# Attention on the FFN's array: two visits per batch through all eight PSUM banks, in place of three visits

## The chip, the cores and the metric

The kernel runs on one NeuronCore of one Trainium2 chip. The metric is device time in microseconds (us) for one execution of the whole program. The kernel before took 302.94 us, the median of three runs (301.93 to 303.04). Engines are named as the profile names them: PE is TensorE's matmul side and PEld its weight load, DVE is VectorE, ACT is ScalarE, POOL is GpSimd (which here only issues loads and a few memsets), and SP is SyncE (which issues transposing DMAs and stores).

## The reference

The inputs are q, k and v of shape (8 batches, 8 heads, 576 positions, 64), w_in (512 x 2048) and w_out (2048 x 512), all fp32; the output is (4608, 512) in fp32. Heads 0 to 3 look at the last 32 positions, heads 4 to 7 at every fourth of the last 128.

```python
scores = q @ k.T / sqrt(64)
rel = pos[:, None] - pos[None, :]
mask_plain = (rel >= 0) & (rel < 32)                        # heads 0 to 3
mask_dil = (rel >= 0) & (rel < 128) & (rel % 4 == 0)        # heads 4 to 7
attn = softmax(where(mask, scores, -1e9))
x = (attn @ v) with the heads side by side, one row per token: (4608, 512)
out = relu(x @ w_in) ** 2 @ w_out
```

## The kernel before

**Two jobs on one array.** Attention of batch b makes the token rows that the FFN (feed-forward network) reads later. Both run in one instruction stream, interleaved by hand: `groups` is the list of FFN groups, and after each group the program runs the attention steps that are due there. Tokens are kept by residue modulo 4 (`RES`), so that dilated heads become dense ones. Heads are handled in pairs e: pairs 0 and 1 are the near heads, pairs 2 and 3 the far (dilated) ones.

**The FFN.** `ffn_groups` cuts the tokens into blocks of 512 columns (the first four of 256). A block of 512 has 32 groups. In the first 16 (`mm1`, line 872) each group is four matmuls of 512 columns into one PSUM tile "pf"; ACT then takes Relu into h2T (line 885) and DVE squares it in place (line 886). In the last 16 (`g2`, line 914), sixteen matmuls for each of four row blocks of 128 tokens read h2T and fill another "pf"; ACT copies it to an `osb` buffer (line 920), of which there are three, and SP stores it (line 841). From group 64 on, the block that starts at group t = 32 (b - 1) is the one beside which batch b is worked on.

**Visits.** From batch `NATURAL` = 3 on, attention uses the array as four quadrants of 64 x 64, in one call of `quadrants` (matmuls at line 601), here called a visit. A visit is given a list `scs` of (batch, pair) whose scores it makes and a list `pvs` whose products with V and whose row sums it makes. It keeps one list of matmuls for each quadrant (g, c), g for the rows and c for the columns, and issues from the quadrant whose streamed columns are fewest. A step that ends in a visit is written `visit(at, scs, pvs)`: it runs after group `at`. Before, batch b has scores of pair 2 at t-8, scores of 3 and products of 2 at t+5, scores of 0 and 1 and products of 3 at t+17, and products of 0 and 1 (with scores of pair 2 of the next batch) at t+24. Batch 3 has them at groups 59, 71, 81 and 88.

**PSUM.** There are eight banks: four "pf" in rotation (`ps_f`, the FFN's), two "pa" (`ps_a`), one "po" and one "pd". A visit's first score pair goes to the two "pa", its first product pair to "po" and "pd"; a second pair of either kind borrows two "pf".

**Around a visit.** After the scores come the steps `E` (ACT's Exp at line 638, DVE's mask at line 640, the `sums` of neighbouring blocks at line 647); after the products `L` (ACT's Ln of the row sums, lines 614 to 620) and `X` (ACT's Exp of the negated Ln at line 624, DVE's multiplication into xT at lines 627 and 629). Before the scores, DVE arranges what arrived: `R` (lines 476 and 479) copies the far heads' block ends, `K` (line 470) and `Q` (line 468) copy the near heads.

**How data arrives.** POOL issues, in a written order (the `PROGRAM` string, then `LOAD_V`, `LOAD_QK`), loads of q and k (line 171, four DMAs a batch: two parts of each), and of V (lines 443, 448 and 455: 24 DMAs a batch, 16 of them rows of the near heads). SP issues four transposing DMAs a batch (`cross`, line 238) from the staged q and k to `qx` and `kx`, between the stores of the FFN. POOL uses eight DMA semaphores in rotation. Each engine works its queue in program order.

The step order within one group number is set by the second entry of the step's tuple; the program sorts on these two:

```python
steps.append((at, 2, b, "V0" + ...))            # a visit
steps.append(((57, 57, 54, 55)[x] if early else t - 14 + x, 1, b, code))   # R
steps.append((t + x if early else t - 6 + x, 1, b, code))                  # K, Q
...
while steps and steps[0][0] <= g:
    natural_step(*steps.pop(0)[2:])
```

Of the kernel before, what the change touches and what calls it, by code (L numbers as in the profile page):

```python
# [12 lines left out]
RES = 4  # L13
# [12 lines left out]
    "X21 M21 L31 X31 M31 E01 E11 | L2:q00123 L2:q10123 L1:v1dpr | | P01 D01 L01 X01 M01 P11 D11 L11 X11 M11 | | "  # L26
    "| | | | | | | | | | m n | | | | | | 1q1 1q3 | 1q2f 1k2f | 1k1a 1v3 | 1a2 | 1v2 1k0a 1q0v | 1o2 | 1a0 1a1 | "
    "1k3 1o0 1o1f | 1a3 1Q0 | 1K0 1o3 | 1Q1 1K1 | 1Q2 | 1b0 | | 1Q3 1K2 L2:vwp L3:q00123 L3:q10123 L2:vwdr | "
    "L2:x | | 2q0 | | 2k0 1V2 | 1b2 1p0 | 1b1 1V3 1K3 | L3:x | 1p2 1p1f | 2a0 1b3 | 2k1l 2b0 2o0 1p3f 2k1h | 2q1 "
    "| | 2p0 L3:V 2a1 | 2b1 | | 2o1 | | | 2p1f L4:q10123 L4:q00123 | | | | L4:x | | | | | | | | | | | | | | | | "  # L30
    "| | L4:V | | | | | | | | | | | L5:q10123 | | | | L5:q00123 | | L5:V | | | | | | L5:x | | | | | | | | "
    "L6:q00123 | | | | | | | | | | | | | L6:q10123"
# [32 lines left out]
def kernel(  # L65
# [109 lines left out]
    def crossed(b: int, e: int):  # L175

        return int(b == XB and e == 3 or b >= NATURAL and e == 1)
# [259 lines left out]
    def load_v_rows(b: int):  # L437


        vds[b] = vd_pool.tile([P, NE // 2, 2, RES * D], bf16, name="vd")  # L440
        for hl, rows in enumerate(sides):
            for e in range(NE // 2):
                nc.gpsimd.dma_start(  # L443
                    vds[b][rows, e, :, :],
                    v[b, H // 2 + 2 * e + hl, 0:512, :].rearrange("(m p r) d -> p m (r d)", p=64, r=RES),
                )
            for i in (0, 8):
                nc.gpsimd.dma_start(  # L448
                    v_rows[b % 2][rows, NE // 2 :, i, :],
                    v[b, H // 2 + hl : H : 2, 64 * i : 64 * i + 64, :].rearrange("h p d -> p h d"),  # L450
                )
            for e in range(NE // 2):
                p0 = sides[hl ^ crossed(b, e)].start
                for r in range(RES):
                    nc.gpsimd.dma_start(  # L455
                        v_rows[b % 2][p0 + 16 * r : p0 + 16 * r + 16, e, :, :],
                        v[b, 2 * e + hl, :, :].rearrange("(i m r) d -> r m i d", r=RES, m=16)[r],
                    )

    def arrange(b: int, what: str, g: int, jj: int):  # L460
# [5 lines left out]
        n = H // 2  # L466
        if what == "Q":
            nc.vector.tensor_copy(q_both[rows, :, jj::2, :], qx[b % 2][src, 0:n, :, :])  # L468
        elif what == "K":
            nc.vector.tensor_copy(  # L470
                k_both[rows, g::2, :, :].rearrange("p i h (c j m) -> p j (h c) i m", c=2, j=2)[:, jj, :, :, :],
                kx[b % 2][src, 0:n, :, :].rearrange("p h c (i m) -> p (h c) i m", m=16)[:, :, g::2, :],
# [17 lines left out]
    def quadrants(scs, pvs):  # L490
# [6 lines left out]
        todo = {(g, c): [] for g in range(2) for c in range(2)}  # L497
        main_s = [ps_a.tile([P, 512], f32, name="pa") for _ in range(2)]

        double = len(pvs) == 2  # L500
        for n, (b, e) in enumerate(pvs):
# [10 lines left out]
            for g, rows in enumerate(sides):  # L512
# [3 lines left out]
                turn_ = hl if (b, e) in turned else 0  # L516
# [41 lines left out]
                for c, bank, items in ((hl, "o", P_), (hl if double else 1 - g, "d", D_)):  # L558
                    for to, lhs, rhs, cols in items[::-1] if g else items:
                        todo[g, c].append(("t" if to is end or to is dend else bank + str(n), to[sides[c]], lhs, rhs, cols))  # L560

        for n, (b, e) in enumerate(scs):
            ps = main_s
            if n:
                pools = ((ps_f, "pf"), (ps_f, "pf")) if pvs else ((ps_o, "po"), (ps_d, "pd"))
                ps = [pool.tile([P, 512], f32, name=name) for pool, name in pools]
            sp[b, e] = ps
            dil = e >= NE // 2
            if double:
                turned.add((b, e))  # L570
            for (g, c), items in todo.items():
                rows, h = sides[g], 2 * e + (c ^ crossed(b, e))
                to = ps[g ^ c if double else g]
                for z in range(4):
                    if dil:
                        x, y = z % 2, 80 * z
                        lhs = kx[b % 2][rows, h, z // 2, 64 * x : 64 * x + 64]
                        rhs = qx[b % 2][rows, h, z // 2, 16 + 48 * x : 96 + 48 * x]
                        out, cols = to[:, y : y + 80], 80
                    else:  # L580
                        i = 2 * z + g
                        lhs, rhs = k_both[rows, i, h, :], q_both[rows, h, :, 16 * i : 16 * i + 24]
                        out, cols = byr(to[:, 96 * z : 96 * z + 96]), 96
                    items.append(("s", out[sides[c]], lhs, rhs, cols))
                if dil:
                    hd = h - H // 2
                    lhs, rhs, y = ends[b % 2][rows, 1, hd, :], byr(ends[b % 2][rows, 0, hd, :]), 320
                elif g == 0:
                    lhs, rhs, y = k_both[rows, 8, h, :], q_both[rows, h, :, 128:M], 384
                if dil or g == 0:  # L590
                    items.append(("s", byr(to[:, y : y + 64])[sides[c]], lhs, rhs, 64))


# [9 lines left out]
    def natural_step(b: int, code: str):  # L603
        what, e = code[0], int(code[1])
        if what in "QKR":
            arrange(b, what, e, int(code[2]))
# [237 lines left out]
    def ffn_groups(tk0: int, nt: int):  # L844
# [6 lines left out]
        kts = (2, 3, 0, 1) if tk0 >= 3 * NT else (0, 2, 1, 3) if NT <= tk0 < 2 * NT else (0, 1, 2, 3) if tk0 in (0, 2 * NT) else (2, 3, 0, 1)  # L851
# [140 lines left out]
    def run(code):  # L992
# [29 lines left out]
        else:  # L1022
            b, what, part, which = int(code[1]), code[3], code[4:5], code[5:]
            if what == "V":
                load_v_rows(b)
# [14 lines left out]
    CROSS = {b: G * (b - 2) + 5 for b in range(6, B)}  # L1040
    LOAD_QK = {b: G * (b - 3) + 6 for b in range(7, B)}
# [11 lines left out]
    for b in range(NATURAL, B):  # L1053
# [5 lines left out]
        def expo(e, *at):  # L1059
            steps.extend((y, 1, b, f"E{e}{x}") for x, y in enumerate(at))  # L1060

        def norm(e, at):
            steps.extend([(at, 3, b, f"L{e}"), (at + 1, 0, b, f"X{e}")])

        start = 59 if early else t - 8
        second = t + (7 if early else 5)
        if early:
            visit(start, [(b, 2)], [(XB, 2), (XB, 3)])
            for e in (2, 3):
                steps.extend([(start + e - 2, 3, XB, f"L{e}"), (start + e - 1, 0, XB, f"X{e}")])  # L1070
        expo(2, *((start + 4, start + 7) if early else (start + 7, start + 9)))
        visit(second, [(b, 3)], [(b, 2)])
        norm(2, second)
        expo(3, second + 3, second + 5)
        visit(t + 17, [(b, 0), (b, 1)], [(b, 3)])
        expo(0, t + 18, t + 18)
        expo(1, t + 18, t + 18)
        norm(3, t + 18)
        visit(t + 24, [(b + 1, 2)] if b + 1 < B else [], [(b, 0), (b, 1)])
        norm(0, t + 24)  # L1080
        norm(1, t + 25)
# [51 lines left out]
```

## Time and profile before

| what | value |
|---|---|
| median of 3 runs (lowest to highest) | 302.94 us (301.93 to 303.04) |
| the profiled execution | 301.97 us, its span 300.2 us |
| granted TensorE clock, mean | 0.998 |
| PE busy | 290.2 us, 3013 matmul records |
| FFN matmuls, lines 872 and 914 | 128.8 us (x695) and 126.6 us (x569) |
| ACT, DVE, POOL busy | 196.1, 162.5, 129.8 us |
| HBM read and written | 37.40 MB and 9.44 MB |

The span runs from the first to the last instruction of the profiled execution; the rest of its time lies around it. A busy row of PE does not say that PE is at its peak, since matmuls overlap and their ends are modelled, so costs on PE are read from starts. A few matmul records are missing from the trace. A wait is named with the line that waited and the line or DMA that ended it.

### The profile page before, as it was taken

The page shows a single profiled execution, that of the slowest core. Times are in us where ns is not written, and L with a number is a line of the kernel's source. Part 1 is how long each engine was busy: PE and PEld are TensorE (multiplying, and loading weights), DVE is VectorE, ACT ScalarE, POOL GpSimd, SP SyncE. Part 2 cuts the span into 40 slices and gives each one's busy share as a digit, 9 for nine tenths or more (in the row PEclk, how much of TensorE's full clock was granted, in tenths as well). Part 3 has the DMA queues.
Part 4 walks back from the last instruction along what each step waited for, and adds up shares of the span by engine and source line. Part 5 has one row for each costly group of instructions (what it writes and reads, how often), then busy time and mean ns, then how long its engine had stood idle before and what let it go on. Part 6 is the DMA issues. An engine that isn't in the chain of part 4 may idle for free.

```text
span 300.2 us, 7580 instructions
## 1 busy us (share of the span) xinstructions
PE 290.2 (97%) x3013; PEld 168.0 (56%) x3045; DVE 162.5 (54%) x477; ACT 196.1 (65%) x417; POOL 129.8 (43%) x210
## 2 busy tenths in 40 slices
PE   8889999999999999999999999999999999999994
PEld 3579756968855554545555455544554455445443
DVE  2675556997858664665467455646564235005300
ACT  6787658859968765776588648865786466126511
POOL 8589883586796893783980386000000000000000
PEclk9999999999999999999999999999999999999999
DMA  7999999999979999999799969303100300121022
GB/s 108 204 175 213 208 151 229 184 169 194 173 86 168 127 174 227 153 155 173 105 148 144 148 98 158 72 17 87 42 0 12 97 35 0 37 71 35 0 72 70
DMA packets 83123, 35.42 MB, mean 118 GB/s; under 512 B 52624, under 2 KB 78480, under 8 KB 83088
## 3 DMA queue, kind: packets, MB, share of 16 engines
q0 software_dynamic: 49280, 18.43, 54.4%
q1 hardware_dynamic: 33120, 16.18, 26.4%
q8 instruction: 24, 0.39, 0.6%
q10 hardware_dynamic: 688, 0.33, 0.4%
q14 instruction: 11, 0.09, 0.1%
HBM read 37.40 MB, written 9.44 MB: 156 GB/s over the span
## 4 chain that ended last, share of the span: by engine, by line
PE 90%; DMA 3%; POOL 2%; issue 2%; ACT 2%; DVE 0%; ACTq 0%; POOLq 0%
PE pf L914 41%; PE pf L872 40%; DMA vd<-in_v_dram 3%; PE po L601 2%; PE pa L601 1%; PE pa L258 1%; PE pd L601 1%; PE pf L601 1%; POOL qb L171 1%; POOL kb L171 1%; ACT rec L809 1%; PE pa L332 1%; ACT h2T L885 1%; PE po L395 1%; PE pd L397 0%
## 5 line engine op out<-in xcount | busy, mean ns | idle before, releaser
L872 PE MATMUL pf<-xT,w_in 128*128 128x512 bf16 (+1 forms) x695 | 128.8, 340 | 1.6 <-ACT rec L809 1.1
L914 PE MATMUL pf<-w_out_sb,h2T 128*128 128x512 bf16 (+2 forms) x569 | 126.6, 373 | 2.4 <-issue 1.9
L872 PEld LDWEIGHTS <-w_in 128*128 128x128 bf16 x704 | 77.4, 113 | 47.1 <-DMA w_in<-in_moe_w_in_dram 1.4
L885 ACT ACTIVATE h2T<-pf 128x512 bf16<-128x512 f32 x144 | 83.2, 600 | 23.3 <-PE pf L872 22.9
L886 DVE TENSOR_TENSOR h2T<-h2T 128x512 bf16<-128x512 bf16 x144 | 59.5, 424 | 56.0 <-ACT h2T L885 53.5
L914 PEld LDWEIGHTS <-h2T 128*128 128x128 bf16 x592 | 55.4, 98 | 61.1
L455 POOL DMA_DIRECT2D vbd<-in_v_dram x80 | 43.7, 562 | 22.8 <-PE pf L601 9.4
L920 ACT COPY osb<-pf 128x512 f32<-128x512 f32 (+1 forms) x36 | 20.7, 576 | 48.5 <-PE pf L914 42.2
L638 ACT ACTIVATE pt<-pa 128x384 bf16<-128x384 f32 (+1 forms) x32 | 15.2, 499 | 9.2 <-PE pa L601 9.2
L627 DVE TENSOR_TENSOR xT<-po,rec 128x512 bf16<-128x512 f32 x16 | 11.1, 692 | 17.2 <-ACT rec L624 16.5
L443 POOL DMA_DIRECT2D vd<-in_v_dram x20 | 12.2, 618 | 10.4 <-PE pa L601 10.4
L624 ACT ACTIVATE rec<-rec 128x576 f32<-128x576 f32 x22 | 15.0, 683 | 0.4
L192 POOL DMA_DIRECT2D vbd<-in_v_dram x16 | 10.9, 690 | 9.4 <-DMA kb<-in_k_dram 3.2
L171 POOL DMA_DIRECT2D qb<-in_q_dram x18 | 13.1, 725 | 1.5 <-POOLq L1117 0.8
L171 POOL DMA_DIRECT2D kb<-in_k_dram x18 | 12.8, 709 | 2.1 <-issue 1.1
L640 DVE TENSOR_TENSOR pt<-pt,mask_f 128x384 bf16<-128x384 bf16 x24 | 8.3, 355 | 9.6 <-ACT pt L638 9.5
L640 DVE TENSOR_TENSOR pt<-pt,mask_n 128x448 bf16<-128x448 bf16 (+1 forms) x20 | 7.0, 372 | 9.8 <-ACT pt L638 9.8
L448 POOL DMA_DIRECT2D vbd<-in_v_dram x20 | 12.1, 623 | 0.1
L620 ACT ACTIVATE rec<-pd 64x512 f32<-64x512 f32 x20 | 11.6, 580 | 0.0
L468 DVE COPY qT<-xx 64x1152 bf16<-64x1152 bf16 x20 | 9.3, 465 | 0.5
L666 PE MATMUL po<-kbd 128*128 128x512 bf16 (+1 forms) x20 | 7.2, 483 | 1.1 <-DVE kbd L936 1.1
L601 PE MATMUL pd<-pt,mk 64*64 64x160 bf16 (+4 forms) x150 | 8.1, 219 | 0.0
(138 smaller groups left out, 299.5 us busy)
## 6 DMA issues: line engine op xcount, KB each, us to landing
qb<-in_q_dram POOLq DMA_DIRECT2D x7, 320.0 KB, 7.0
kb<-in_k_dram POOLq DMA_DIRECT2D x7, 320.0 KB, 10.5
vd<-in_v_dram POOLq DMA_DIRECT2D x32, 64.0 KB, 6.6
w_in<-in_moe_w_in_dram POOLq DMA_DIRECT2D x4, 512.0 KB, 8.4
w_out_sb<-in_moe_w_out_dram POOLq DMA_DIRECT2D x4, 512.0 KB, 12.2
out_dram<-osb SPq DMA_DIRECT2D x16, 128.0 KB, 3.5
qb<-in_q_dram POOLq DMA_DIRECT2D x7, 256.0 KB, 7.5
kb<-in_k_dram POOLq DMA_DIRECT2D x7, 256.0 KB, 7.4
```

Of the source, the lines that this page charges most:

```text
L171: nc.gpsimd.dma_start(t[0:n, part, hs, :], src[b, hs, t0 : t0 + RES * n, :].rearrange("h (p r) d -> p h (r d)", r=RES))
L443: nc.gpsimd.dma_start(vds[b][rows, e, :, :], v[b, H // 2 + 2 * e + hl, 0:512, :].rearrange("(m p r) d -> p m (r d)", p=64, r=RES),)
L455: nc.gpsimd.dma_start(v_rows[b % 2][p0 + 16 * r : p0 + 16 * r + 16, e, :, :], v[b, 2 * e + hl, :, :].rearrange("(i m r) d -> r m i d", r=R ...
L601: nc.tensor.matmul(out, lhs, rhs, start=begin, stop=True, skip_group_check=True)
L624: nc.scalar.activation(rec[:, :], rec[:, :], ACT.Exp, scale=-1.0)
L638: nc.scalar.activation(pt, sp[b, e][g][:, 0:n], ACT.Exp, scale=SCALE)
L640: nc.vector.tensor_tensor(out=pt, in0=pt, in1=mask, op=ALU.mult)
L872: nc.tensor.matmul(to, w_in_sb[piece][:, kt, c0 : c0 + 509 : 4], rhs, start=(kt == kts[0] and x == 0), stop=(kt == kts[-1] and x == per - ...
L885: nc.scalar.activation(hv, acc[u][:, :].rearrange("p (x n) -> p x n", x=per), ACT.Relu)
L886: nc.vector.tensor_tensor(out=hv, in0=hv, in1=hv, op=ALU.mult)
L914: nc.tensor.matmul(cur[m][:, c0:c1], h2[:, f, P * m : P * m + P], w_out_sb[:, f, c0:c1], start=(f == 0), stop=(f == NF - 1),)
L920: (nc.vector.tensor_copy if last and part == 1 else nc.scalar.copy)(osb[:, c0:c1], cur[m][:, c0:c1])
```

## The change

From batch 3 on, a batch has two visits instead of three. One stands at t+15, between the block's last `mm1` group and its first row block, the other at t+23, between its second and third row block. Each makes the scores of two pairs (one far, one near) and the products of two pairs (one far, one near), and so fills all eight banks: the far scores in the "pa", the near scores in two "pf", the far products in "po" and "pd", the near products in the other two "pf". Batch 3 has one more visit, at group 71, with the scores of pair 0 alone; the last visit has products alone.

In `quadrants`, each quadrant now first gets the second score pair and the first product pair, and then the first score pair and the second product pair. The near pairs 0 and 1 both have their heads crossed (`crossed`), so that the far products load two quadrants and the near ones the other two.

What feeds the visits moves: `arrange` copies K and Q pair by pair, in 16 steps instead of 8 per batch, those of pair 0 from t-26 on; `R` moves from t-14 to t-31 (t-20 for batch 4); the transposes of batches 6 and 7 move from t-27 to t-40, and those of batch 5 from after group 101 to after group 88; q and k of batch 4 are issued before the V rows of pair 1 of batch 3; q and k of batch 7 are issued before V of batch 6. The FFN's contraction order for the blocks from token 1536 on goes from (2, 3, 0, 1) to (2, 0, 3, 1).

```diff
-    "| | 2p0 L3:V 2a1 | 2b1 | | 2o1 | | | 2p1f L4:q10123 L4:q00123 | | | | L4:x ...
-    "| | L4:V ... | L5:q10123 | | | | L5:q00123 | | L5:V | ... | L5:x ... "L6:q00123 | ... | L6:q10123"
+    "L3:Vd0 L4:q00123 L4:q10123 L3:V1 2a1 | 2b1 | | 2o1 | | | 2p1f | | | | L4:x ...
+    "| L4:V | | L5:q10123 | L5:q00123 | ... | L5:x | ... | L5:V | | | | | L6:q00123 | L6:q10123"
...
-        return int(b == XB and e == 3 or b >= NATURAL and e == 1)
+        return int(b == XB and e == 3 or b >= NATURAL and e < NE // 2)
...
-        todo = {(g, c): [] for g in range(2) for c in range(2)}
+        todo = {(g, c): [[], []] for g in range(2) for c in range(2)}
+        for n, (b, e) in reversed(list(enumerate(scs))):
+            ps = main_s
+            if n:
+                pools = ((ps_f, "pf"), (ps_f, "pf")) if pvs else ((ps_o, "po"), (ps_d, "pd"))
+                ps = [pool.tile([P, 512], f32, name=name) for pool, name in pools]
+            swap = double and n == 0
+            for (g, c), (one, two) in todo.items():
+                items = two if n == 0 else one
...
+                        todo[g, c][n].append(("t" if to is end or to is dend else bank + str(n), ...))
+        todo = {gc: one + two for gc, (one, two) in todo.items()}
...
-        kts = (2, 3, 0, 1) if tk0 >= 3 * NT else ...
+        kts = (2, 0, 3, 1) if tk0 >= 3 * NT else ...
...
-    CROSS = {b: G * (b - 2) + 5 for b in range(6, B)}
-    LOAD_QK = {b: G * (b - 3) + 6 for b in range(7, B)}
+    CROSS = {b: G * (b - 1) - 40 for b in range(6, B)}
+    LOAD_QK = {b: G * (b - 3) - 4 for b in range(7, B)}
...
-        visit(second, [(b, 3)], [(b, 2)])
-        visit(t + 17, [(b, 0), (b, 1)], [(b, 3)])
-        visit(t + 24, [(b + 1, 2)] if b + 1 < B else [], [(b, 0), (b, 1)])
+            visit(71, [(b, 0)], [])                  # batch 3 only
+        visit(t + 15, [(b, 3), (b, 1)], [(b, 2), (b, 0)])
+        expo(b, 1, t + 15, t + 15)
+        norm(b, 0, t + 15)
+        expo(b, 3, t + 16, t + 16)
+        norm(b, 2, t + 17)
+        visit(t + 23, [] if last else [(b + 1, 2), (b + 1, 0)], [(b, 3), (b, 1)])
+            expo(b + 1, 0, t + 23, t + 23)
+        norm(b, 3, t + 23)
+        norm(b, 1, t + 24)
+            expo(b + 1, 2, t + 27, t + 29)
+        at = t - 20 if b == NATURAL + 1 else t - 31
...
+                elif e:
+                    to = t - 8 + x
+                else:
+                    to = t - 16 + x - x // 7 if b == NATURAL + 1 else t - 26 + x
+                steps.append((to, 1, b, f"{code}{e}"))
```

## The prediction

> **What bounds the kernel now.** I read the page first, then the PE timeline around every array visit, then the queues that feed the visits (SP's timeline, the DMA landings, DVE's timeline). A "visit" below is one call of `quadrants`; "group n" is the n-th FFN group, the unit in which the program counts its places.
>
> ```profile
> span 300.2 us, 7580 instructions
> PE 290.2 (97%) x3013; PEld 168.0 (56%) x3045; DVE 162.5 (54%) x477; ACT 196.1 (65%) x417; POOL 129.8 (43%) x210
> PEclk9999999999999999999999999999999999999999
> DMA  7999999999979999999799969303100300121022
> PE 90%; DMA 3%; POOL 2%; issue 2%; ACT 2%; DVE 0%; ACTq 0%; POOLq 0%
> ```
>
> PE is 97% busy at full granted clock and holds 90% of the chain of waits. Other engines have room on average. The DMA engines are full over about the first 60% of the span, which is where the batches 3 to 6 get their data. So two things can move the time: what the visits cost on PE, and a load or copy that arrives after PE wants it. The PE timeline around the visit at group 101, with start, duration, line, operation and count:
>
> ```profile
> 88.06 7.07 PE L872 MATMUL pf<-xT,w_in 128*128 128x512 bf16 x32
> ...
> 118.52 5.54 PE L872 MATMUL pf<-xT,w_in 128*128 128x512 bf16 x23
> 124.00 0.22 PE L601 MATMUL po<-pt,vd 64*64 64x80 bf16 x1
> ...
> 124.50 0.21 PE L601 MATMUL pa<-kbd 64*64 64x64 bf16 x4
> 124.64 8.83 PE L872 MATMUL pf<-xT,w_in 128*128 128x512 bf16 x39
> 133.31 1.89 PE L914 MATMUL pf<-w_out_sb,h2T 128*128 128x512 bf16 x8
> ```
>
> An FFN matmul of 512 columns starts every (7.07 - 0.38) / 31 = 0.216 us, so a group of four takes 0.863 us and PE streams 512 / 0.216 = 2,374 columns per us. The last matmul before the visit starts at 118.52 + 5.54 - 0.38 = 123.68 and the next at 124.64. The visit costs 124.64 - 123.68 - 0.22 = 0.74 us, and 0.03 more because the first block matmul behind it runs long: 0.77 us. The same reading (where a visit is followed by L914, one record is missing: 27 rows for 28 matmuls) gives 0.97 us for the visits at t+17, 1.10 at t+24, and 0.91 for the last one, which has no scores. Two of the t+24 visits are 0.07 (at 142.1) and 0.33 us (at 172.7) longer. Nothing else stops PE between 88 and 290 us.
>
> **The visits, worked out.** From `quadrants` I count the columns that the busiest quadrant streams: 1,152 at t+5, 1,664 at t+17, 1,824 at t+24, 1,440 in the last. Divided by 2,374 these are 0.49, 0.70, 0.77 and 0.61 us, so each visit pays a fixed 0.27 to 0.33 us. That is what merging can save. A new full visit holds scores of a far and a near pair (384 + 448 columns) and a far product pair (1,536) in its busiest quadrant: 2,368 columns, 1.00 us, with the fixed part 1.27 to 1.33. I take 1.30.
>
> Before, from group 64: 5 x 0.77 + 5 x 0.97 + 4 x 1.10 + 0.91 + 0.40 of waits = 14.4 us. After: nine full visits (groups 79 and 87, 111 and 119, 143 and 151, 175 and 183, 207) 11.7, the scores alone of pair 0 of batch 3 at group 71 (448 columns, 0.19 + 0.28) 0.47, the last visit (1,536 columns) 0.95: 13.1 us. Gain 1.3 us, from 1.0 to 1.6 by the bounds of the fixed part. The 0.40 of waits goes because the `R` copies move from t-14 to t-31: at 142.1 and 172.7 the scores waited for them.
>
> **All eight banks.** The block behind a visit now takes the bank that the near scores filled first, so it waits for that Exp.
>
> ```profile
> 133.51 0.60 ACT L885 ACTIVATE h2T<-pf 128x512 bf16<-128x512 f32 x1 [0.27 <-PE pf L872]
> 135.95 0.93 ACT L638 ACTIVATE pt<-pa 128x448 bf16<-128x448 f32 x2 [1.84 <-PE pa L601]
> ```
>
> The last L872 matmul before 133.31 starts at 133.09; its Relu runs from 133.51 to 134.11. A visit in that place would start 0.31 us behind that matmul, at 133.40; the Relu ends 0.70 us into it. The Exp of 448 columns overlaps its predecessor by 0.1 us and takes 0.54: it ends 1.15 us into the visit, and DVE rows follow ACT ends by 0.03. PE wants the bank at 1.30 - 0.09 - 0.03 = 1.18. So the border costs nothing to 0.05; I take 0.02, 0.2 us for nine. If the Exp had to await the visit's last matmul (as at 135.95, 0.08 behind it) it would be 0.5 each, 4.5 us. The second product pair needs the bank of that Relu after 1,664 columns, 0.70 us in: a tie as well. At t+23 the osb copy (0.585) stands in the Relu's place with the same figures.
>
> The Trainium skill, TensorEngine Tiling (Array Packing), section PSUM Bottleneck, speaks against this: array tiling speeds up TensorE but not the emptying of PSUM. By that rule alone, with both Exps of 0.93 us on the path at nine borders, the change would lose 8 us on top; the rows above say that the emptying fits under the visit.
>
> **The copies and loads that move.** DVE gets 16 half copies for 8 whole ones (Q 0.46, K 0.29 to 0.32 whole; I take 0.21 a half), under 1 us more a batch; the Ln count falls. Both are covered by idle time (DVE works 18 of 31 us between 118.5 and 149.3). The order of the contraction steps is free, as all of X is long done. On POOL, L4:q passes eight V rows of about 0.55 us, so it is issued 4.5 us sooner, near 82.5. The eight V rows it passes still land before 95 and are read at 111. L7:q passes V of batch 6, at a time when POOL waited anyway (2.0 us at 135.99); V of batch 6 waits for the visit at group 119 and is out near 157, read near 193. On SP, the transposes of batch 5 pass the stores of two row blocks, and with three osb buffers no copy needs those before 137 us. These cost nothing; without that cover a block's copy would hold a bank.
>
> The moved step that matters is `R` of batch 5, from group 114 to group 97, near 120 us, ahead of 14 squares (L886) on DVE. It reads the second part of both transposes:
>
> ```profile
> 105.86 14.26 SPq L841 DMA_DIRECT2D out_dram<-osb  x10
> 120.31 1.29 SPq L238 DMA_TRANSPOSE xx<-kb  x1
> 121.71 1.87 SPq L238 DMA_TRANSPOSE xx<-qb  x1
> 123.68 3.15 SPq L238 DMA_TRANSPOSE xx<-kb  x1
> 126.96 2.25 SPq L238 DMA_TRANSPOSE xx<-qb  x1
> ...
> xx<-qb SPq DMA_TRANSPOSE x1, 4.6
> ```
>
> The last transpose is issued at 126.96 and lands 4.6 us later, at 131.5. The first starts when its K load lands (issued 110.14, 10.0 us to landing). That load keeps its place behind the same 52 DMAs on POOL from 71.7 us, so it comes no sooner by much; POOL near 107.4 and two stores fewer beside it give me 129.7 for the last landing. DVE would then stand from 120 to 129.7, with the squares of groups 98 to 111 behind it. The squares are read by L914 only, after the visit at group 111.
>
> ```profile
> 170.98 0.19 DVE L476 COPY kbd<-xx 64x128 bf16<-64x128 bf16 x1 [1.85 <-DMA xx<-qb]
> 171.09 0.30 DVE L479 COPY kbd<-xx 64x128 bf16<-64x128 bf16 x1
> 171.41 0.69 DVE L627 TENSOR_TENSOR xT<-po,rec 128x512 bf16<-128x512 f32 x1
> ...
> 159.13 0.76 DVE L886 TENSOR_TENSOR h2T<-h2T 128x512 bf16<-128x512 bf16 x2
> ```
>
> The first row shows that such a wait happens already. An `R` costs 171.41 - 170.98 = 0.43, a square in a queue 0.76 - 0.42 = 0.34. After landing DVE owes 4 x 0.43 + 14 x 0.34 + 8 x 0.21 = 8.2 us. PE reaches the block at 88.06 + 48 x 0.863 + 0.47 + 3 x 1.30 = 133.9 and its sixteenth matmul at 137.1. A landing up to 128.9 is free; each us after costs PE one. At 129.7 it costs 0.8 us; at 131.5, 2.6. The six sets of four transposes from 53.7 us on took 8.7, 13.6, 12.3, 11.2, 20.0 and 9.8 us; from a start near 119 the shortest ends at 127.7 and costs nothing. Batch 4 (`R` at group 76, landing near 101) and batch 6 (free until 159.7, from a start near 143.5) have slack.
>
> Sum: -1.3 + 0.2 + 0.8 = -0.3 us. The profiled run took 301.97 (span 300.2, 1.8 around it), 0.97 under the median of 302.94; set against the median, 302.6.
>
> **Rivals.** (1) Transposes early enough, or held up nowhere: only the visits count, -1.1, up to -1.6: 301.8. For it: the 8.7 us set. Against it: the DMA row is full there. (2) Slower: `R` of batch 5 on DVE holds the squares for longer. Price one us per us from 128.9; it decides, by more than 0.5%, from a landing at 131.5 on (2.6 - 1.1 = 1.5). At 132.3, with half copies at the 0.33 of a whole one, it is 3.4 + 1.0 - 1.1 = 3.3: 306.2, and a set as long as that of batch 6 before (20.0) would add as much again. For it: the load is no earlier on its queue. (3) The eight banks: 4.5 - 1.3 = 3.2 slower, plus 0.8: 306.9. For it: nothing between visit and block is spare. Against it: the scores that free the bank come first in the visit.
>
> **Chances.** Forecast 0.48, rival 1 0.22, rival 2 0.22, rival 3 0.08. About 0.5% is what a measurement can tell from no change: 301.4 to 304.5. Faster: 0.10 of rival 1 and 0.02 of the forecast. Slower: 0.17 of rival 2, 0.06 of rival 3, 0.05 of the forecast. The range from 301.3 to 305.8 leaves out about 0.08 below and 0.12 above.
>
> **What would show it.** Thirteen visits for seventeen; nine of them 1.27 to 1.33 us from matmul to matmul; the first L914 behind a visit without a wait on L638; the waits of L601 near 142 and 172 gone; DVE idle on xx from 120 to 130, then squares in a row, and L914 waiting for L886 by under 1 us near 136. Visits of 1.8 us, or a DVE wait past 132, would prove me wrong.

## The result, and the profile after

The changed kernel takes 310.49 us (median of six runs, 308.91 to 312.35) where the kernel before, run beside it, takes 302.50 (six runs, 301.83 to 303.04): a ratio of 1.0257, 95% interval 1.0221 to 1.0292. The forecast was 302.6, its range ended at 305.8. Medians, here and below, are of all runs, while the ratios leave out the runs that were over 1.5% above the fastest of their kernel (one of e1, three of e5, two of e11, one of e12, one of the kernel before beside e9 and e10), so that a ratio need not be the quotient of two medians. The profiled execution took 308.91 us against 301.97, so 6.9 us have to be found. The page of the changed kernel:

```profile
span 307.1 us, 7602 instructions
PEclk9999999999999999999999999999999999999999
DMA  7999999999999899999994069402200210021022
PE 71%; DMA 11%; POOL 8%; DVE 5%; issue 2%; ACT 1%; POOLq 0%; ACTq 0%
```

PE's share of the chain fell from 90% to 71%: PE now waits where before it hardly did. The clock is not the reason in this execution (mean 0.998 in both). In three of the other five executions its mean was 0.992 to 0.995, and these took 310.98 to 312.35 us; the three at 0.998 or more took 308.91 to 309.99. So a part of the 8.0 us between the medians may be clock, in executions that were not profiled. The chain of waits in order of time (start, duration, what) shows what it runs through between 111 and 133 us, where the chain of before held PE's own matmuls alone:

```profile
111.22 9.50 DMA kb<-in_k_dram
...
127.76 4.61 DMA xx<-qb
132.39 0.36 DVE kbd L477
132.91 0.57 DVE h2T L890 x2
```

The load of K of batch 5, its transposes, the `R` copies, and then the squares: the steps that the prediction feared. The timeline of SP and that of DVE (start, duration, line, operation, count, wait before it):

```profile
111.86 2.58 SPq L845 DMA_DIRECT2D out_dram<-osb  x3
120.86 1.25 SPq L237 DMA_TRANSPOSE xx<-kb  x1
122.21 1.82 SPq L237 DMA_TRANSPOSE xx<-qb  x1
124.13 3.53 SPq L237 DMA_TRANSPOSE xx<-kb  x1
127.76 1.66 SPq L237 DMA_TRANSPOSE xx<-qb  x1
```

```profile
120.54 0.61 DVE L469 COPY qT<-xx 64x576 bf16<-64x576 bf16 x2
...
132.39 0.36 DVE L477 COPY kbd<-xx 64x128 bf16<-64x128 bf16 x1 [10.10 <-DMA xx<-qb]
132.50 0.41 DVE L480 COPY kbd<-xx 64x128 bf16<-64x128 bf16 x1
132.74 0.74 DVE L890 TENSOR_TENSOR h2T<-h2T 128x512 bf16<-128x512 bf16 x2
...
136.77 0.36 DVE L471 COPY kbd<-xx 64x320 bf16<-64x320 bf16 x1
```

The transposes land at 127.76 + 4.61 = 132.4, and DVE stands still for 10.1 us. On PE the block behind the visit at 136.6 then meets squares that are not done (the brackets: the idle time before, and what ended it):

```profile
138.82 2.10 PE L918 MATMUL pf<-w_out_sb,h2T 128*128 128x512 bf16 x9
141.11 0.39 PE L918 MATMUL pf<-w_out_sb,h2T 128*128 128x512 bf16 x1 [0.18 <-DVE h2T L890]
141.91 0.39 PE L918 MATMUL pf<-w_out_sb,h2T 128*128 128x512 bf16 x1 [0.40 <-DVE h2T L890]
142.70 0.39 PE L918 MATMUL pf<-w_out_sb,h2T 128*128 128x512 bf16 x1 [0.41 <-DVE h2T L890]
```

From start to start, less 0.216 a matmul, these waits come to 1.62 us. That is not the largest part. A full visit, on the PE timeline:

```profile
134.15 2.54 PE L876 MATMUL pf<-xT,w_in 128*128 128x512 bf16 x11
136.62 0.39 PE L605 MATMUL pf<-qT,kbd 64*64 64x96 bf16 x18
...
136.99 0.20 PE L605 MATMUL po<-pt,vd 64*64 64x80 bf16 x1
137.12 0.43 PE L605 MATMUL pf<-pt,vbd 64*64 64x64 bf16 x2
137.36 0.21 PE L605 MATMUL pa<-pt,vbd 64*64 64x64 bf16 x1
...
138.16 1.04 PE L918 MATMUL pf<-w_out_sb,h2T 128*128 128x512 bf16 x3
```

The last block matmul before the visit starts at 134.15 + 2.54 - 0.38 = 136.31, the next at 138.16: by the prediction's reading the visit costs 138.16 - 136.31 - 0.216 + 0.03 = 1.67 us, not 1.30. In its middle, where the first products of the near pair stand (pf<-pt,vbd), no matmul starts for 0.13 and then for 0.24 us, though matmuls of this size start 0.01 to 0.03 apart elsewhere. No engine is named as the cause. The instructions of the visit's line in that window, grouped by kind (count, duration in ns, first and last start), show what PE's queue did:

```profile
L605 PEldq EVENT_SEMAPHORE  x4: 51/51/51, 136.9 to 137.2; - x4
```

Four instructions that only wait for semaphores. In the trace they start at 136.91, 137.02, 137.14 and 137.25, 0.11 to 0.13 apart, and name six of POOL's eight DMA semaphores, on which the near pair's V rows had landed long before (the last one by 111): nothing was waited for, yet each takes its turn in the queue. The kernel before has such instructions too, at its visit of 142.14:

```profile
L601 PEldq EVENT_SEMAPHORE  x6: 51/51/51, 141.1 to 141.8; - x6
```

There the near pair's products came first in the visit, so the waits stood ahead of it and ran while the FFN matmuls in front of them still streamed.

The sum of the 6.9 us, in the profiled execution: nine full visits at 0.37 over the forecast 1.30, 3.3; waits of visits for DVE at groups 71 (1.0), 87 (0.7) and 119 (0.4), 2.1; the squares 1.6; the visit at group 59 costs 1.99 instead of 1.12, 0.9; PE comes to its first visit 0.5 later (81.0 against 80.4; in the profiles of the other runs below that start lies anywhere between 80.3 and 82.3, so it belongs to the sum of these two executions but is not put down to the change). That is 8.4, less the 1.3 that merging saves: 7.1. PE's rows of the view of waits, with us in total, times and the longest, name the copies:

```profile
PE pa L605 <- DVE qT L469: 0.8, 1, 0.8
PE pa L605 <- DVE kbd L480: 0.7, 1, 0.7
PE pf L605 <- DVE qT L469: 0.4, 1, 0.4
```

The first row is the visit at 71 and the third that at 87, which wait for `Q`; the second is the visit at 59, where the scores of batch 3 (pa<-kbd) used to be last in the stream and now stand ahead of the second pair's products, before their `R` copies are done. The visit at 119 has no row here: its products start at 147.28 and 147.41, 0.05 behind the two steps of `X` that read the banks of the visit before out (they end at 147.23 and 147.36).

### The profile page after: what moved, and what is told of

It is laid out like the page before. It is cut to its first block, busy times and chain, and to the rows that moved or that the text cites. A ratio compares the mean times of both kernels' runs of the same rounds, so it can differ in the third digit from the quotient of the medians.

```text
span 307.1 us, 7602 instructions
## 1 busy us (share of the span) xinstructions
PE 294.5 (96%) x3017; PEld 170.0 (55%) x3045; DVE 167.5 (55%) x507; ACT 192.3 (63%) x397; POOL 129.5 (42%) x210
## 4 chain that ended last, share of the span: by engine, by line
PE 71%; DMA 11%; POOL 8%; DVE 5%; issue 2%; ACT 1%; POOLq 0%; ACTq 0%
PE pf L918 32%; PE pf L876 32%; DMA w_in<-in_moe_w_in_dram 5%; POOL vbd L456 3%; DMA kb<-in_k_dram 3%; DVE h2T L890 2%; PE pf L605 2%; DMA xx<-qb 1%; DMA vbd<-in_v_dram 1%; PE pa L257 1%; POOL vbd L448 1%; POOL qb L170 1%; POOL vbd L191 1%; POOL vd L443 1%; POOL kb L170 1%
## 5 line engine op out<-in xcount | busy, mean ns | idle before, releaser
L918 PE MATMUL pf<-w_out_sb,h2T 128*128 128x512 bf16 (+2 forms) x570 | 128.2, 373 | 2.3 <-DVE h2T L890 1.0
L642 ACT ACTIVATE pt<-pa 128x384 bf16<-128x384 f32 (+1 forms) x24 | 11.2, 490 | 7.2 <-DVE xT L633 7.2
L631 DVE TENSOR_TENSOR xT<-po,rec 128x512 bf16<-128x512 f32 x11 | 7.6, 692 | 14.6 <-ACT rec L628 14.6
L170 POOL DMA_DIRECT2D qb<-in_q_dram x18 | 13.2, 735 | 1.9 <-DMA qb<-in_q_dram 1.1
L477 DVE COPY kbd<-xx 64x128 bf16<-64x128 bf16 x24 | 5.5, 229 | 15.5 <-DMA xx<-qb 15.0
L469 DVE COPY qT<-xx 64x576 bf16<-64x576 bf16 x40 | 12.4, 310 | 0.6
L471 DVE COPY kbd<-xx 64x320 bf16<-64x320 bf16 (+1 forms) x40 | 10.5, 263 | 0.7
L631 DVE TENSOR_TENSOR xT<-pf,rec 128x512 bf16<-128x512 f32 x11 | 7.6, 691 | 5.1 <-ACT rec L628 5.1
```

The source lines that it names most:

```text
L170: nc.gpsimd.dma_start(t[0:n, part, hs, :], src[b, hs, t0 : t0 + RES * n, :].rearrange("h (p r) d -> p h (r d)", r=RES))
L631: nc.vector.tensor_tensor(out=tok[:, :, 16:M], in0=byr(o[:, :]), in1=byr(rec[:, 0:512]), op=ALU.mult)
L918: nc.tensor.matmul(cur[m][:, c0:c1], h2[:, f, P * m : P * m + P], w_out_sb[:, f, c0:c1], start=(f == 0), stop=(f == NF - 1),)
```

## The experiments

Four causes were put up: W, the four semaphore waits of PE's queue in each full visit; D, the `R` copies of batch 5 holding DVE; Q, the late copies of batches 3 and 4; S, the order of the scores at group 59. The rival to W was B, a wait for one of the eight banks. One table has what each kernel's trace gave, by the reading above (us; "block" is the sum of the waits of the block behind group 111), then median and ratio to the kernel before with its 95% interval. A full visit is one that waits for no other engine; the traces are of one execution each, not of the median one. Line numbers shift by some 6 to 14 in some kernels.

| run | full visit | 59 | 71 or 73 | 87 | block | median | ratio |
|---|---|---|---|---|---|---|---|
| the change | 1.67 to 1.71 | 1.99 | 1.44 | 2.35 | 1.62 | 310.49 | 1.0257 [1.0221, 1.0292] |
| e1_touch | 1.31 | 1.55 | 1.52 | 2.93 | 3.07 | 310.53 | 1.0261 [1.0191, 1.0332] |
| e2_scores_last | 1.56 to 1.65 | 1.11 | 1.40 | 3.07 | 3.43 | 310.29 | 1.0227 [1.0173, 1.0281] |
| e3_late_copies | 1.67 to 1.71 | 1.72 | 1.40 | 2.57 | 0 | 306.84 | 1.0115 [1.0068, 1.0162] |
| e4_batches34 | 1.67 to 1.83 | 1.59 | 0.44 | 2.03 | 5.48 | 312.31 | 1.0282 [1.0215, 1.0348] |
| e5_all_four | 1.48 | 1.25 | 0.44 | 1.47 | 0 | 303.90 | 1.0010 [0.9979, 1.0042] |
| e6_touch_constant | 1.68 to 1.84 | 2.15 | 1.61 | 2.22 | 2.15 | 310.69 | one run |
| e7_touch_late | 1.31 | 1.71 | 1.44 | 3.09 | 0 | 304.67 | 1.0063 [1.0035, 1.0090] |
| e9_best | 1.31 | 1.11 | 0.44 | 3.77 | 0.06 | 303.76 | 1.0008 [0.9976, 1.0040] |
| e10_best_no_touch | 1.67 to 1.71 | 1.11 | 0.44 | 2.72 | 0 | 306.35 | 1.0117 [1.0071, 1.0163] |
| e11_best_second | 1.31 | 1.11 | 0.44 | 2.03 | 0 | 303.21 | 0.9999 [0.9970, 1.0028] |

**e1_touch.** One matmul of 16 columns on the near pair's V rows, at the head of each full visit, so that PE meets the four waits there.

```diff
         todo = {gc: one + two for gc, (one, two) in todo.items()}
+        for b, e in pvs:
+            if b >= NATURAL and e < NE // 2:
+                nc.tensor.matmul(
+                    op[pvs[0]][0][:, 0:16], v_rows[b % 2][:, e, 0:2, :].rearrange("p i d -> p (i d)"), ones[:, 0:16],
+                    start=True, stop=True, skip_group_check=True,
+                )
```

> The changed kernel with one more matmul at the head of each visit for a near product pair: 128 x 128 weights taken from two blocks of that pair's V rows, 16 columns, into the bank of the first product pair, which is written over later. It makes PE wait for the eight DMAs of those V rows before the visit instead of in its middle. Theory W (PE's own semaphore instructions, about 0.11 us each, stand in the middle of a visit, 0.37 us in nine of them): the pauses of 0.13 and 0.23 us behind the 39th matmul of a visit go, a full visit falls from 1.67 to about 1.35 to 1.45 us with the touch included, and the time falls by 2 to 3 us. Theory B (the pause is the wait for the bank that the last Relu or copy still reads): the pause stays where it is, visits become 0.05 to 0.1 us longer, the time rises by up to 1 us.

The same visit in its timeline, and the waits of the touch's line:

```profile
134.32 1.89 PE L882 MATMUL pf<-xT,w_in 128*128 128x512 bf16 x8
136.04 0.17 PE L600 MATMUL po<-mk,vbd 128*128 128x16 bf16 x1
136.15 0.39 PE L611 MATMUL pf<-qT,kbd 64*64 64x96 bf16 x18
...
137.33 1.04 PE L924 MATMUL pf<-w_out_sb,h2T 128*128 128x512 bf16 x4
```

```profile
L600 PEldq EVENT_SEMAPHORE  x4: 51/51/51, 133.4 to 133.8; - x4
```

The visit costs 137.33 - 135.83 - 0.216 + 0.03 = 1.31 us with one matmul more, and the last of the four waits (133.77) now runs 2.3 us ahead of it, under the FFN matmuls. W holds for the visits and B falls: the banks are the same. The median did not move; in the trace an earlier PE waits longer for DVE (3.07 in the block, 2.93 at 87).

**e6_touch_constant.** The control: the same matmul, on a constant.

```diff
-                    op[pvs[0]][0][:, 0:16], v_rows[b % 2][:, e, 0:2, :].rearrange("p i d -> p (i d)"), ones[:, 0:16],
+                    op[pvs[0]][0][:, 0:16], ident, ones[:, 0:16],
```

> A control to the touch: the same 16-column matmul at the head of each full visit, but on the constant identity matrix, whose load no later instruction waits for. If the pauses are the four waits for the V rows' loads that stand in TensorE's queue ahead of the near pair's first product, they stay where they are: full visits 1.68 to 1.72 us, 0.37 of it in two pauses behind the 39th or 40th matmul. Rival (any matmul ahead of the visit shortens it, for instance since it takes over the wait for a bank or the change of tile size): 1.32 as in the run with the touch on V rows. The time by the first: that of the changed kernel, 309 to 312.

The visits stayed at 1.68 or above, and the two pauses in their place. It is what the touch reads that helps, not that it is there.

**e2_scores_last.** The first score pair (n = 0, the far one; two expectations below call it the near pair) goes behind the products in each quadrant's list.

```diff
-            for (g, c), (one, two) in todo.items():
-                items = two if n == 0 else one
+            for (g, c), (one, _, three) in todo.items():
+                items = three if n == 0 else one
...
-        todo = {gc: one + two for gc, (one, two) in todo.items()}
+        todo = {gc: one + two + three for gc, (one, two, three) in todo.items()}
```

> The changed kernel with the first score pair put last in each quadrant, behind the second product pair. Theory S (in the visit at group 59 the scores come too early in two quadrants and wait 0.85 us for the R copies of batch 3): that visit falls from 1.96 us to about 1.1 us as before the change, the full visits stay at 1.67 us, and the time falls by about 0.9 us. Rival (the visit at 59 is late because its product operands are late): its price stays near 1.9 us.

S holds: 1.11 us at group 59. Most full visits came to 1.56: of the two pauses the second stayed, 0.22 us from start to start, with two of the four waits in it.

**e3_late_copies.** All `R` copies of batches from 4 on at t-20, `K` and `Q` of pair 0 at t-16 and after (the change has that for batch 4 alone).

```diff
-        at = t - 20 if b == NATURAL + 1 else t - 31
+        at = t - 20
...
-                    to = t - 16 + x - x // 7 if b == NATURAL + 1 else t - 26 + x
+                    to = t - 16 + x - x // 7
```

> The changed kernel with R and the copies of K and Q of pair 0 of batches 5 to 7 on the places that batch 4 has (R from t-20, K and Q from t-16 to t-10) instead of t-31 and t-26. Theory D (DVE stands 10 us on the last transpose of batch 5 and the squares behind it arrive late, 1.5 us on PE near 141 us): DVE's longest wait on xx falls below 4 us, the row block behind group 111 no longer waits for L890, and the time falls by 1 to 2 us. Against it stands the risk that Q of pair 0 is now late for the visit at t-9, as it is for batch 4 (0.65 us): then up to 0.65 us for each of batches 5 to 7 comes back and the time stays within 1 us of the changed kernel's.

The transposes landed no sooner (133.1), but DVE had no long wait on xx and the block none at all. The median fell by 3.6 us, and the intervals of the two ratios do not meet. The profiled executions differ by 2.4: 1.6 in the block, 0.4 at the visit of 119, and 0.4 by which PE came earlier to its first visit. The rest of the 3.6 lies in executions of the change that were not profiled, and what it is stays open.

**e4_batches34.** Against Q: the lone visit of batch 3 at group 73, its Exps at 74 and 76, and the eight copies of pair 0 of batch 4 in two groups.

```diff
-            visit(71, [(b, 0)], [])
-            expo(b, 0, 73, 75)
+            visit(73, [(b, 0)], [])
+            expo(b, 0, 74, 76)
...
-                    to = t - 16 + x - x // 7 if b == NATURAL + 1 else t - 26 + x
+                    to = t - 16 + x // 4 if b == NATURAL + 1 else t - 26 + x
```

> The changed kernel with the scores-only visit of batch 3 two groups later (73, its Exps at 74 and 76), and the copies of K and Q of pair 0 of batch 4 all at t-16 and t-15, ahead of the multiplication of pair 2 into xT. Theory Q (DVE copies of Q are late for two visits: 0.97 us at group 71, 0.65 us at group 87): both waits on L469 go, the visit at 73 costs about 0.5 us, that at 87 about 1.67, and the time falls by about 1.5 us. Rival (DVE is simply behind in this stretch): the wait only moves, to the visits at 79 and 87 or to the squares, and the time stays within 0.7 us of the changed kernel's.

The lone visit cost 0.44 and waited for nothing, so the wait at 71 was Q. The rest got worse: batch 5's transposes landed at 134.8, the block waited 5.48 us, and then the clock fell (the profiled execution, 313.60, is the longest of the four). The windows of the view by stretches (from and to, then busy time and instruction counts of PE, PEld, DVE, ACT and POOL, the granted clock, DMA share, GB/s):

```profile
137.00:143.60 6.60, 3.78 (x12) 0.96 (x10) 6.19 (x21) 1.54 (x4) 2.59 (x4) 1.00 1.35 180
143.70:150.50 6.80, 6.25 (x15) 2.09 (x15) 4.65 (x15) 2.25 (x5) 0.00 (x0) 0.50 1.47 185
```

**e7_touch_late.** The two main causes together, the edits of e1 and e3.

> The two main causes taken away together and nothing else: the touch on V rows, and the R copies at t-20 with K and Q of pair 0 at t-16.. for every batch from 4 on. The late copies alone gave 306.8. If the pauses are worth what the trace shows, 9 x 0.35 = 3.2 us go: 303.6, full visits at 1.32, no block waits behind 111, DVE without a long wait on xx. With up to 0.8 us more waiting for Q at group 87, since PE is there sooner: 304.4. Rival (the time saved in visits comes back whole in waits for DVE or Q, as it did with the touch alone): 306.5 to 307, with 3 us of waits to be found.

304.67 instead of 306.84 for e3 alone, 2.2 us of the 3.2 that the visits gave, though the intervals of the two ratios overlap; the visit at 87 took 0.5 of the rest, waiting for `Q` (1.07 and 0.42 us in the timeline's brackets).

**e5_all_four.** The edits of e1, e2 and e3 together, the lone visit at 73 with Exps at 74 and 75, and pair 0's copies at t-16 + x//4 in every batch.

> All four edits in one kernel: the 16-column matmul on the near pair's V rows at the head of each full visit, the scores behind the products of the stream, the R copies at t-20 with K and Q of pair 0 at t-16 + x//4 for every batch from 4 on, and the scores of pair 0 of batch 3 at group 73 with their Exps at 74 and 75. If the four causes are all there is and add up, from 310.5: full visits 9 x 0.35 = 3.2 us, the visit at 59 0.9, the squares about 3.6 of the median (measured with the late copies alone), the wait at 71 about 1.0; that would be 301.8, with visits of 1.32, no block waits, and 1.0 to 1.1 at group 59. Against the sum: with batch 4's R copies ahead of the mask of pair 0 the visit at group 79 may keep a wait of 0.5 and that at 87 one of 0.5 to 1.2, which gives 302.8 to 303.5. Rival (a PE that is earlier only waits longer for DVE or for Q, as in the run with the touch alone): 306 to 307, with the gain returned in waits at 79, 87 and in the block behind 111.

No visit and no block waits for DVE any more, and the ratio is 1.001: the four causes together hold the loss of the change. It came 0.4 us above what was expected against the sum, and for another reason than written: each full visit cost 1.48, 0.16 more than with the touch alone, one pause that ends 0.05 us behind the Relu or osb copy which frees the borrowed bank.

**e9_best and e10_best_no_touch.** The far scores behind the products only at group 59; then the same without the touch.

```diff
-            for (g, c), (one, _, three) in todo.items():
-                items = three if n == 0 else one
+            for (g, c), (one, two, three) in todo.items():
+                items = one if n else three if pvs and pvs[0][0] < NATURAL else two
```

> The version with all four edits, but with the scores behind the products only in the visit at group 59; in the visits of batches from 3 on the near pair's scores stand ahead of the products again. The 0.15 us that each full visit there spent behind its first far pair, waiting for the bank of the last Relu or osb copy, should go: 1.32 instead of 1.48, nine times 0.16 = 1.4 us. 303.9 - 1.4 = 302.5, ratio to the kernel before 0.995 to 1.000. Rival (the scores in front wait for the Q copies, as they did at groups 79 and 87 with the late copies): 303.5 to 304, with those two visits at 2 us or more.

> The same version without the touch, so that the touch alone is measured where nothing else holds PE up. If the four waits in TensorE's queue are what the change costs, nine full visits go from 1.32 to 1.67 to 1.70 us: 3.1 to 3.4 us longer than with the touch, 305.6 to 305.9 (ratio about 1.008 to 1.010 to the kernel before). Rival (what the waits cost is slack that something else takes up anyway): within 1 us of the version with the touch.

The touch is worth 2.6 us by the medians and 1.1% by the ratios, whose intervals do not meet: W is shown in time as well. But e9 was no faster than e5. Its visits are 1.31, and the visit at 87 costs 3.77, where the rival there said 2 or more. In e9's view of waits and its windows:

```profile
PE po L600 <- DVE xT L639: 2.0, 1, 2.0
```

```profile
108.00:110.00 2.00, 2.00 (x11) 0.88 (x9) 1.95 (x9) 0.96 (x3) 1.72 (x4) 1.00 0.17 11
110.00:112.50 2.50, 0.62 (x3) 0.10 (x1) 2.43 (x8) 1.78 (x5) 2.50 (x5) 1.00 0.58 42
112.60:114.20 1.60, 1.60 (x105) 1.49 (x106) 0.49 (x2) 1.06 (x3) 1.60 (x3) 0.76 0.86 136
114.20:117.00 2.80, 2.80 (x12) 1.04 (x8) 1.72 (x7) 2.54 (x6) 2.55 (x5) 0.53 1.18 208
```

PE, ahead of time, waits 2.36 us from start to start for `X` of the visit at 79, which empties the bank "po" and stands on DVE behind four `Q` copies and a wait for batch 4's transposes (until 104.3), and pays again at half clock. Three of its twelve runs took 301.2 to 301.7, the others 302.4 to 305.3; only one was profiled, so whether those three missed this wait stays open.

**e11_best_second.** `X` of the far pair one group earlier, and the far scores behind the products at 87 too.

```diff
-                items = one if n else three if pvs and pvs[0][0] < NATURAL else two
+                items = one if n else three if pvs and pvs[0][0] < min(b, NATURAL + 1) else two
...
-        norm(b, 2, t + 17)
+        norm(b, 2, t + 16)
```

> The best version so far lost 2.45 us at the visit of group 87, where the products waited for the X rows of visit 79, which stood behind four Q copies on DVE, and the scores for these Q copies; behind that wait the block's matmuls stood 0.427 apart for 2.5 us, another 1.2 us. Two edits: the Ln and X of the far pair one group earlier (so that X stands ahead of the Q copies), and the near pair's scores behind the products in the visit at 87 too. If that is where its time went, visit 87 costs 1.5 to 2.0 us, the clock stays at full, and the median falls by 1.5 to 2.5 us to 301.3 to 302.3, ratio 0.992 to 0.998. Rival (the wait is set by the landing of batch 4's transposes, near 104, and only changes its name): 303 to 304, with 2 us or more at 87 again.

The clock stayed full and the visit at 87 fell to 2.03, but that at 119 now waited 0.95, most of it for `Q`. Ratio 0.9999. No version of the merged visits beat the kernel before. From the third visit on, e11's cost 14.9 us with 0.7 and 0.95 of waits in them, so 13.2 without, against 14.7 before: by the traces merging does save 1.5 us, and the waits for copies take it. No time shows that saving by itself.

**e8_before_early_copies and e12_before_early_r.** The early `R` copies in the kernel before, with the transposes (in e12 the loads too) moved for them. In e8 the transposes of batch 5 stood ahead of that batch's loads (and one part of batch 6's too), so it computes those scores from older rows.

> One part of the change alone, in the kernel before: the transposes of batch 5 at group 89 (before: 93) and the R copies of batches from 5 on at t-31 (before: t-14), with the two short visits that every pair of pairs had kept. If it is this move that makes DVE stand and hold the squares, the block at group 111 waits for L890's counterpart here (L886) by 1.5 to 3.5 us, DVE waits about 10 us on xx for batch 5, and the two waits of the scores of 0.07 and 0.33 us near 142 and 172 go: 302.5 + 1.5 to 3.5 - 0.4 = 303.6 to 305.6. Rival (DVE is late only because of the merged visits and what they ask of it): 302.1, no block waits.

316.03 us, ratio 1.0418 [1.0368, 1.0468], but without a wait near 133: the transposes of batch 5, which waited for no load, landed at 122.8. So it does not answer for batch 5. At batch 6, though, it shows a chain that e12 will show again: DVE waits 6.22 us for a transpose, ACT's Exp 5.59 for an `X` on DVE, and PE up to 5.0 for a Relu behind that Exp (a row each of DVE's timeline, ACT's timeline and PE's waits).

```profile
161.09 0.19 DVE L466 COPY kbd<-xx 64x128 bf16<-64x128 bf16 x1 [6.22 <-DMA xx<-qb]
165.99 0.49 ACT L628 ACTIVATE pt<-pa 128x384 bf16<-128x384 f32 x1 [5.59 <-DVE xT L619]
PE pf L862 <- ACT h2T L875: 9.2, 2, 5.0
```

In e12 the loads stand in front (their places in `PROGRAM`, too, are those of the change; that part of the edit is left out here):

```diff
-    CROSS = {b: G * (b - 2) + 5 for b in range(6, B)}
-    LOAD_QK = {b: G * (b - 3) + 6 for b in range(7, B)}
+    CROSS = {b: G * (b - 1) - 40 for b in range(6, B)}
+    LOAD_QK = {b: G * (b - 3) - 4 for b in range(7, B)}
...
-            steps.append(((57, 57, 54, 55)[x] if early else t - 14 + x, 1, b, code))
+            steps.append(((57, 57, 54, 55)[x] if early else t - 14 + x if b == NATURAL + 1 else t - 31 + x, 1, b, code))
```

> One part of the change alone in the kernel before, now with the loads in front of what reads them: the loads of batch 5 at groups 81 and 82, its transposes at 89, the loads of batch 6 at 101 and 102, the transposes and loads of the later batches as in the change, and the R copies of batches from 5 on at t-31 instead of t-14. The visits, the K and Q copies and PSUM are those of the kernel before. If the early R copies are what makes DVE hold the squares, DVE waits about 10 us for batch 5's transposes (until 131 to 132.5) and the block behind group 111 waits for the squares (L886) by 1.0 to 3.5 us; the two waits of the scores of 0.07 and 0.33 us go: 302.7 + 1.0 to 3.5 - 0.4 = 303.3 to 305.8. More, up to 308, if TensorE's clock falls behind it. Rival (DVE is late only with the split copies and the merged visits of the change): 302.3 to 302.7, no waits of L914 for L886.

It took 314.50 us, ratio 1.0342 [1.0264, 1.0419]: far above the expectation, by the mechanism expected and one link more. From its profile, the longest of its four runs (316.09): a row of DVE's timeline, waits of ACT and PE, and the clock:

```profile
136.50 0.19 DVE L466 COPY kbd<-xx 64x128 bf16<-64x128 bf16 x1 [12.37 <-DMA xx<-qb]
```

```profile
ACT pt L628 <- DVE xT L619: 11.9, 2, 11.1
PE pf L862 <- ACT h2T L875: 9.7, 1, 9.7
```

```profile
PEclk9999999999999999975999999999999999999999
```

Behind the `R` copies on DVE stands not only the squaring but an `X`, whose last step reads a bank of scores (xT<-pa), and ACT's next Exp (pt<-pa) waits for it; behind that Exp stand the Relus, and PE stops for 9.7 us, then runs at half clock for a while. So the early `R` copies, with the loads and transposes moved for them, cost the kernel before at least about as much as the whole change does. In the changed kernel ACT waited for an `X` too, by 4.5 us at the longest, and PE for the squares by 1.6. Why it is hurt less was not tried: its `X` steps come at other groups, and its last transpose landed at 132.4, that of e12 at 136.5.

## Why the prediction was wrong

**Right: the columns.** Where nothing else stands in the visit, the count held: 1.31 us with the touch for a forecast of 1.30, 0.94 for the last visit (0.95), 0.44 for the scores alone (0.47). The two waits of the scores near 142 and 172 went.

**Right: the Exp at the border; missed: the bank that `X` empties.** Rival 3 was refuted: visits of 1.31 leave no room for an Exp on the path. The rule of the Trainium skill, TensorEngine Tiling (Array Packing), section PSUM Bottleneck, that the prediction weighed (tiling does not speed up the emptying of PSUM) did not bind there. It did bind elsewhere: 0.16 us a visit in e5, where the far scores stand last and the pause ends with a Relu or an osb copy, and once 0.66 in e2, behind an osb copy; and PE waited for `X` to empty "po", 0.4 us at group 119 in the change and 2.36 at 87 in e9. The prediction and its rivals had no term for the wait on `X`.

**Wrong: "2,368 columns, 1.00 us, with the fixed part 1.27 to 1.33".** The step that failed took a fixed part from the old visits and did not ask what else stands in PE's queue, and where. The old rows held the same semaphore waits, ahead of the visit. Moving the near products into the middle of a visit moved the waits too: a visit of 1.67 in place of 1.30, of which 0.36 us, 3.2 us in nine, are these waits, as the visits of e1 against the change and of e10 against e9 measure them (2.6 us in the medians of the second two). The prediction's own list of signs had "visits of 1.8 us" as proof against it; 1.67 without any other wait is nearer to that than to 1.33.

**Wrong in size: `R` of batch 5.** Forecast, a landing at 129.7 and 0.8 us; it was 132.4, later than before (131.5). The load of K was not sooner but later (issued at 111.22, before at 110.14), so the "two stores fewer" bought nothing; rival 2's "the load is no earlier on its queue" was the right reading. The half copies cost 0.30 (`Q`: 0.61 for two) and 0.22 to 0.36 (`K`), not 0.21. And the price of one us per us from 128.9, which gives 3.5 for this landing, was no price: it counted the squares alone and a PE that is on time. In the changed kernel PE came to the block 4.3 us later than forecast (138.16 against 133.9) and lost 1.6 there; removing the cause gave 3.6 in e3's median, near the 3.5 by luck; in e12 PE's stop behind such copies was 9.85. Rival 2's conditions came true (a landing past 131.5, half copies near 0.3), but its 306.2 lies 4.3 under the measured time: it had neither PE's semaphore waits nor the late `Q` copies.

**Missed: DVE's order for batches 3 and 4.** "Both are covered by idle time" was judged by DVE's sum over 31 us, not by each copy's due time. The `Q` copies were late at 71 and 87, and `R` at 59, where the new order of the scores took away what had covered it: 2.6 us together. Batch 4's "slack" was true of its `R` copies and not of the `Q` copies behind them.

## What to carry to other kernels

When work moves within an engine's queue, move its wait instructions too in the estimate: waits for things that landed long ago are free only while something queued in front of them still runs, and a small matmul that reads the same data earlier can take them there. When a copy that waits for a transfer is put earlier in an in-order queue, list everything behind it to the first step that another engine needs (here an `X` that ACT's next Exp waits for, behind which Relus stand), and price that, not the copy. Idle time in an engine's sum covers nothing by itself; each moved step has a time at which it is due.

## What the runs showed of the hardware

Four semaphore waits in PE's queue, each 51 ns long and 0.11 to 0.13 us from the next, cost 0.36 us when they stand between short matmuls (the change, visits of 1.67), and nothing that shows when they run 2.3 us ahead under queued ones (e1, 1.31).

The granted TensorE clock fell to half after PE had waited, and stayed there for about 3.4 us in e9 (0.8 us of the third and 2.6 of the fourth of its rows above, by their clocks of 0.76 and 0.53) and 6.8 us in e4, where PE was busy 57% of the 6.6 us before, with no two matmul starts more than 0.91 apart. The share alone does not decide: in e1 PE was busy 57% of 4.5 us (first row), in e2 70% of 7.0 (second), and both kept their clock:

```profile
139.00:143.50 4.50, 2.58 (x9) 0.63 (x7) 4.22 (x13) 0.36 (x1) 0.00 (x0) 1.00 1.59 187
137.00:144.00 7.00, 4.90 (x67) 1.79 (x55) 6.59 (x21) 2.23 (x6) 1.47 (x3) 1.00 1.37 181
```

The Trainium skill, TensorE: Matmul & The Clock Gate, Part 1: The HAM clock gate, has the clock at half after an idle window of about 3.4 us. These rows agree on the half and show shorter stops that were enough: one of 2.36 us in e9, and many short ones in e4. The half clock makes a wait on PE dearer than it looks: in e9, by estimate, 1.7 us (half of the 3.4) on top of the 2.36.
